# Soft-capped attention and a squared-ReLU MLP in one kernel: pads that set addresses, smaller weight loads, and decode work moved between engines and stages

## The chip, the cores and the metric

The kernel runs on one core of one Trainium2 chip. The metric is the device time of one execution in microseconds, less is better. TensorE does the matrix products, VectorE (DVE in the rows) and ScalarE (ACT) the elementwise work, GpSimd (POOL) and SyncE (SP) issue transfers. TensorE's granted clock is 1.00 (its 2.4 GHz level) over the whole span of the profiled execution.

## The reference, cut to what matters

Inputs are float32, except that the expert weights arrive as float64 words, which the kernel decodes itself.

```
q, k, v: (4, 12, 448, 64)                       # batch, heads, sequence, head size
scores = q @ k^T / 8;  scores = cap * tanh(scores / cap)
attn = exp(scores - max);  attn = attn / (sum(attn) + 1e-09)
x = (attn @ v), heads side by side              # (1792, 768)
h = relu(x @ w_in)                              # w_in  (768, 2048)
out = (h * h) @ w_out                           # w_out (2048, 768)
```

## The kernel before

The work has three stages, and inside a stage the order of the instructions on every engine is written out by hand.

**Attention.** 24 pairs of heads (a batch and two heads each), one iteration n of the loop in `tile_softcap_attention_mlp` for each, and a last one, n = 24, for what is left. In iteration n TensorE makes the scores of pair n (three products and, for every second pair, a fourth "half" one for two pairs), then, for pair n-1, the product with v (`pv_half`, `pv`, into the PSUM tile `pa`) and the sums of the row (`sums`, into `pb`). Both PSUM tiles exist once, so `pv_half` of a pair waits until `evac` of the pair before has copied `pa` away. ScalarE does tanh and exp. VectorE adds the exps (`add_p`, `add_p3`), transposes q and k (`turn_kq`), copies the sums out (`take_sums`), adds the guard 1e-9 to them and takes the reciprocal (`invert`), scales (`normalise`) and copies `pa` out (`evac`). The sums travel in a chain: `take_sums` copies them from PSUM, a transfer of SP gathers them into `cmp`, `invert` works on that small tile, SP stores it to DRAM, and `spread` on POOL loads it back over all partitions, three iterations later; `normalise` then multiplies. For the first two batches (pairs 0 to 11) `normalise` also splits its result into a rounded high part (a cast, line 503) and a low part (a subtraction, line 504).

**Weights inside the attention.** Column f of w_in (128 of its 2048 columns) is loaded by one transfer of 768 KB (`fetch_w`) and decoded in six steps: size and rest on ScalarE, clip, shift, sign and total on VectorE (lines 40 to 48); then its two halves are split into high and low operands (lines 557 and 558). `early_work` is a generator that yields after every step; the loop takes one step in an iteration from n = 4 and two from n = 10. Four columns are decoded there, three of them also split.

**First product.** Sixteen columns of w_in times x, as a Strassen scheme on blocks: for each pair of columns p seven products, each of 18 matmuls of 448 columns, all on line 345. Left operands are weights in the pool `w`. The moving operands x lie in five pools: B11 and B21 in `xab` (also products 1 and 2), B22 in `xg0` (product 3), T2 in `xg1` (product 6), B12 and later T1 in `xg2` (product 5), T3 and T4 in `xf` (products 7 and 4). A list scheduler (`Plan`) with written costs and due times puts the instructions of this stage in order; the rooms it gives out (raw tiles, decoded tiles, operands) are tokens. Columns 2 and 3 enter it as already decoded tiles.

**Second product.** Strassen again: 49 products of 24 matmuls of 384 columns on line 1124, with the squared h loaded back from DRAM (`load_a`), split into operands (lines 1113 and 1114) two products ahead, and fetched five products ahead (`LEAD`).

**Addresses.** Pools are laid out one behind the other. A pad (`shift`) is a tile that is never used and only moves what comes after it. `lctx` holds `xab`; `rctx` holds a pad, then `w`, a pad, `xf`, and further pools up to `xg0`; `xg1` and `xg2` are laid from the other end of the memory, behind `pad3`; the operand pool of the second product likewise, behind `pad4`. Tiles in these pools are whole multiples of 256 bytes in each partition, so that the distance between an x tile and a left operand, taken modulo 256 bytes, is the same for all tiles of a pool. In the layout before, x minus left operand is 192 for `xab`, 64 for `xf` and `xg0`, and 32 for `xg1` and `xg2`; in the second product it is 160 and 64.

## Time and profile before

| | |
|---|---|
| time, median of 3 runs | 597.59 us (596.75 to 599.28) |
| profiled execution: its time, its span | 595.01 us, 593.5 us |
| TensorE busy | 580.0 us (98%) |
| weight loads busy | 458.5 us (77%) |
| VectorE busy | 472.9 us (80%) |
| ScalarE busy | 375.5 us (63%) |
| GpSimd busy | 156.0 us (26%) |

The span runs from the first to the last instruction of the profiled execution; about 1.5 us of its own time lie outside. Attention ends at 172.6 us, where the first matmuls of the first product start; the second product runs from 384.2 to 588.4 us. Busy shares are averages over the three stages, which have different limits, so each stage has to be read alone. A busy TensorE isn't TensorE at its fastest: the distance from one matmul's start to the next one's is read from the timeline.

### The profile page before, as it was taken

The page shows a single profiled execution, that of the slowest core. Times are in us where ns is not written, and L with a number is a line of the kernel's source. Part 1 is how long each engine was busy: PE and PEld are TensorE (multiplying, and loading weights), DVE is VectorE, ACT ScalarE, POOL GpSimd, SP SyncE. Part 2 cuts the span into 40 slices and gives each one's busy share as a digit, 9 for nine tenths or more (in the row PEclk, how much of TensorE's full clock was granted, in tenths as well). Part 3 has the DMA queues.
Part 4 walks back from the last instruction along what each step waited for, and adds up shares of the span by engine and source line. Part 5 has one row for each costly group of instructions (what it writes and reads, how often), then busy time and mean ns, then how long its engine had stood idle before and what let it go on. Part 6 is the DMA issues. An engine that isn't in the chain of part 4 may idle for free.

```text
span 593.5 us, 9080 instructions
## 1 busy us (share of the span) xinstructions
PE 580.0 (98%) x3286; PEld 458.5 (77%) x3286; DVE 472.9 (80%) x646; ACT 375.5 (63%) x428; POOL 156.0 (26%) x245
## 2 busy tenths in 40 slices
PE   8998999999999999999999999999999999999996
PEld 5333333333348999999999999999999999999996
DVE  2878999999979898898787877734999998676661
ACT  5999788889976887686765757554833643323230
POOL 8687977777421000120211112100000000000000
PEclk9999999999999999999999999999999999999999
DMA  9999978979216233888878768979799618555611
GB/s 134 133 187 187 166 132 161 156 126 186 76 45 196 86 119 126 276 269 269 254 235 287 245 209 338 284 248 343 192 308 300 155 42 231 165 143 157 174 40 45
DMA packets 138678, 110.18 MB, mean 186 GB/s; under 512 B 53408, under 2 KB 127648, under 8 KB 138624
## 3 DMA queue, kind: packets, MB, share of 16 engines
q1 hardware_dynamic: 125088, 71.86, 48.0%
q0 software_dynamic: 12000, 37.39, 23.1%
q8 instruction: 27, 0.44, 0.4%
q10 hardware_dynamic: 1536, 0.27, 0.3%
q14 instruction: 27, 0.22, 0.2%
HBM read 82.84 MB, written 26.56 MB: 184 GB/s over the span
## 4 chain that ended last, share of the span: by engine, by line
PE 42%; issue 32%; DMA 8%; POOL 7%; DVE 6%; ACT 2%; SPq 2%; DVEq 0%; POOLq 0%
PE po L1124 30%; PE pa L455 4%; PE sc L397 4%; POOL g_dram L700 3%; DMA kqn<-in_k_dram 2%; POOL w_dram L1013 2%; PE pa L439 2%; POOL kqn L354 2%; DMA a<-g_dram 2%; ACT p L415 1%; DVE add L430 1%; DMA vn<-in_v_dram 1%; DMA kqn<-in_q_dram 1%; DVE kq L390 1%; PE pb L448 1%
## 5 line engine op out<-in xcount | busy, mean ns | idle before, releaser
L1124 PE MATMUL po<-th,gh 128*128 128x384 f32 x728 | 189.8, 336 | 0.0
L1124 PE MATMUL po<-th,gl 128*128 128x384 f32 x392 | 131.8, 336 | 0.2 <-DVE gl L1114 0.2
L1124 PEld LDWEIGHTS po<-th,gh 128*128 128x128 f32 x728 | 131.8, 188 | 0.0
L1113 ACT CAST gh<-a 128x1024 fp32r<-128x1024 f32 x47 | 49.4, 1051 | 96.7 <-PE po L1124 76.4
L345 PE MATMUL hps<-xt,op 128*128 128x448 f32 x450 | 93.9, 365 | 0.0
L345 PEld LDWEIGHTS hps<-xt,op 128*128 128x128 f32 x450 | 84.3, 187 | 7.0
L415 ACT ACTIVATE p<-sc 128x896 f32<-128x896 f32 x84 | 73.2, 909 | 19.6 <-PE sc L397 19.5
L1114 DVE TENSOR_TENSOR gl<-a,gh 128x1024 fp32r<-128x1024 f32 x47 | 57.5, 1222 | 23.2 <-ACT gh L1113 23.2
L1124 PEld LDWEIGHTS po<-th,gl 128*128 128x128 f32 x392 | 73.7, 188 | 0.5 <-DVE gl L1114 0.5
L423 ACT ACTIVATE p<-p 128x1792 f32<-128x1792 f32 (+1 forms) x48 | 72.5, 1510 | 1.4
L345 PE MATMUL hps<-xs,op 128*128 128x448 f32 x324 | 68.3, 365 | 0.0
L345 PEld LDWEIGHTS hps<-xs,op 128*128 128x128 f32 x324 | 60.6, 188 | 6.1 <-ACT p L415 0.7
L397 PE MATMUL sc<-kq 64*128 64x448 f32 x288 | 60.7, 554 | 0.5 <-DVE qks L530 0.5
L354 POOL DMA_DIRECT2D kqn<-in_k_dram x92 | 59.0, 647 | 7.4 <-DVE cmp L473 2.3
L455 PE MATMUL pa<-p,vn 128*64 128x448 f32 x288 | 59.4, 548 | 0.0
L397 PEld LDWEIGHTS sc<-kq 64*128 64x128 f32 x288 | 25.7, 186 | 34.6 <-issue 24.0
L345 PE MATMUL hps<-xh,op 128*128 128x448 f32 x168 | 49.6, 363 | 0.0
L379 POOL DMA_DIRECT2D vn<-in_v_dram x48 | 35.4, 741 | 31.9 <-PE pa L455 30.1
L455 PEld LDWEIGHTS pa<-p,vn 128*64 128x64 f32 x288 | 18.5, 136 | 30.9 <-issue 30.9
L48 DVE CUSTOM_DVE_ANT_0 wf<-wraw,wf 128x1536 uint16<-128x1536 uint16 x32 | 30.4, 951 | 5.6 <-ACT wraw L43 3.1
L1137 DVE TENSOR_TENSOR osb<-s,po 128x384 f32<-128x384 f32 x27 | 14.9, 552 | 25.0 <-PE po L1124 25.0
L40 ACT ACTIVATE wf<-wraw 128x768 f32<-128x768 f32 x32 | 29.0, 907 | 8.0 <-DMA w_dram<-wf 6.0
(95 smaller groups left out, 842.3 us busy)
## 6 DMA issues: line engine op xcount, KB each, us to landing
a<-g_dram SPq DMA_DIRECT2D x56, 512.0 KB
wraw<-in_moe_w_in_dram SPq DMA_DIRECT2D x16, 768.0 KB
wraw<-in_moe_w_out_dram SPq DMA_DIRECT2D x16, 768.0 KB
g_dram<-r POOLq DMA_DIRECT2D x18, 448.0 KB, 5.6
g_dram<-u POOLq DMA_DIRECT2D x14, 448.0 KB, 3.6
w_dram<-wf POOLq DMA_DIRECT2D x16, 384.0 KB, 6.4
vn<-in_v_dram POOLq DMA_DIRECT2D x48, 112.0 KB, 4.4
e<-rd POOLq DMA_DIRECT2D x48, 112.0 KB, 3.3
```

The costliest lines, as they stand in the source:

```text
L40: size=lambda: nc.scalar.activation(out=magf, in_=high.bitcast(F32), func=ACTF.Abs, scale=2.0 ** 16),
L48: total=lambda: V.tensor_tensor(out=mag, in0=mag, in1=low, op=ALU.add),
L345: nc.tensor.matmul(out=out, lhsT=w, rhs=x[:, j], start=start and c == 0 and s == 0, stop=stop and c == NHALF - 1 and s == 2, skip_group_ch ...
L354: queue.dma_start(out=kqn[n % NKQ][32 * a:32 * a + 32, i], in_=x)
L379: nc.gpsimd.dma_start(out=vn[n % NKV][r, at:at + NS], in_=x[i::2].rearrange("t r d -> r t d"))
L397: nc.tensor.matmul(out=sc[:, h, :S], lhsT=kt[r, keys(n, h, u)], rhs=qt[r], start=True, stop=True)
L415: nc.scalar.activation(out=p, in_=probs[n, u][:, :, :S], func=ACTF.Tanh, scale=by["qks"])
L423: nc.scalar.activation(out=p, in_=p, func=ACTF.Exp, scale=by["cap"])
L455: nc.tensor.matmul(out=pvs[n, 0][r], lhsT=vn[n % NKV][:, v_slot(n, h, u)], rhs=p[:, h], start=False, stop=(u == NU - 1))
L1113: last["act"] = nc.scalar.copy(out=hi, in_=x)
L1114: last["dve"] = nc.vector.tensor_sub(out=lo, in0=x, in1=f32(hi))
L1124: last["mm"] = nc.tensor.matmul(out=po, lhsT=w[:, c], rhs=m[:, cols], start=(c == 0 and i == 0), stop=(c == HF - 1 and i == 2))
```

## The change

- Two pads grow or are added: `pad0` of 32 words (128 bytes) ahead of `xab`, and `pad1` from 16 to 112 words ahead of `w`. `pad3` shrinks by 8 words (32 bytes), `pad4` grows by 32 words (128 bytes). x minus left operand becomes 64 modulo 256 for all five pools of the first product; in the second product it stays at 160 and 64, with the operands themselves at other places.
- w_in's first four columns are loaded in six transfers of 128 KB each, two in an iteration, from the iterations in `FETCH` (6, 9, 14, 18), in place of one of 768 KB.
- Three columns are decoded in the attention, not four, from n = 9 on, with the number of steps for each iteration in the list `DECODE`. Column 3 is only loaded there; its decode becomes part of the first product's plan.
- The guard is added in `take_sums`, by the instruction that copies the sums out of PSUM; the addition of line 472 goes.
- The cast of line 503 becomes a ScalarE copy one iteration later (`split_high`), and the subtraction follows it (`split_low`).
- B22's split is done for both batches at once in place of one by one.
- Six in place of five tiles of h are loaded ahead of the second product, and those of its first 14 products are fetched two products earlier. The pools of that stage wait for single tiles instead of whole pools when they reuse memory (`by_tile`).

```diff
+    shift(lctx, "pad0", 32)
     xab = lctx.enter_context(tc.tile_pool(name="xab", bufs=NQ))
-    shift(rctx, "pad1", 16)
+    shift(rctx, "pad1", 112)
...
     def take_sums(n):
         e = ep.tile([P, S], F32, tag="es", name="es", bufs=1)
-        nc.vector.tensor_copy(out=e, in_=pvs.pop((n, 1)))
+        nc.vector.tensor_scalar(out=e, in0=pvs.pop((n, 1)), scalar1=guard, scalar2=None, op0=ALU.add)
...
     def invert(n):
         cmp = rds[n]
-        nc.vector.tensor_scalar(out=cmp, in0=cmp, scalar1=guard[:NC], scalar2=None, op0=ALU.add)
         nc.vector.reciprocal(out=cmp, in_=cmp)
...
         nc.vector.tensor_mul(out=x, in0=e[:, 0], in1=e[:, 1])
-        if half:
-            return
-        if b == 0:
-            t = xab.tile([P, 2, 2, S], F32R, tag="x", name="xs")
-            xs.setdefault(("B11", "B21")[i], {})[c] = t[:, 0], t[:, 1]
-        hi, lo = (t[:, b] for t in xs[("B11", "B21")[i]][c])
-        nc.vector.tensor_copy(out=hi, in_=x)
-        nc.vector.tensor_sub(out=lo, in0=x, in1=hi.bitcast(F32))
+        if not half:
+            whole[n] = x, ("B11", "B21")[i], c, b
+
+    def split_high(n):
+        if n in whole:
+            x, name, c, b = whole[n]
+            if b == 0:
+                t = xab.tile([P, 2, 2, S], F32R, tag="x", name="xs")
+                xs.setdefault(name, {})[c] = t[:, 0], t[:, 1]
+            nc.scalar.copy(out=xs[name][c][0][:, b], in_=x)
+
+    def split_low(n):
+        if n in whole:
+            x, name, c, b = whole.pop(n)
+            hi, lo = (t[:, b] for t in xs[name][c])
+            nc.vector.tensor_sub(out=lo, in0=x, in1=hi.bitcast(F32))
...
+    def fetch_early(n):
+
+        for f, at in enumerate(FETCH):
+            if at <= n < at + NHALF:
+                if n == at:
+                    raws[f] = new_raw(scr, 2)
+                for c in (2 * (n - at), 2 * (n - at) + 1):
+                    nc.sync.dma_start(out=raws[f][:, c * P:(c + 1) * P], in_=w_in[c * P:(c + 1) * P, f * P:(f + 1) * P])
...
-    START, DEEP = 4, 3
+    START, DEEP = 9, 3
+    FETCH = 6, 9, 14, 18
+    DECODE = 1, 2, 2, 1, 2, 3, 2, 2, 1, 2, 3, 2, 2, 3, 2, 0
...
         if n >= START:
-            decode_on(1 + (n >= 10))
+            decode_on(DECODE[n - START])
+        split_high(n - 5)
...
             take_sums(n - 1)
-            fetch_wanted()
+            fetch_early(n)
             pv(n - 1)
...
             normalise(n - 4)
+        split_low(n - 5)
         if old:
             evac(n - 1)
...
-    shift(tctx, "pad3", 24, side="right", **by_tile)
+    shift(tctx, "pad3", 16, side="right", **by_tile)
...
-        raw=[(0.0, i, p) for i, p in enumerate((left, left, right))],
-        f=[(0.0, i, right) for i in range(2)],
+        raw=[(0.0, i, p) for i, p in ((1, left), (2, right))],
+        f=[(0.0, 0, left), (0.0, 1, right), (0.0, 3, right)],
...
+    columns[1, 1] = round_column(True, 3, due[6, 1] - 5.0, 40.0, raw3)
...
-    d22 = [split_x("B22", c, [one(x22[c], j) for j in range(2)], due["u", 0, 1], [(), (normal[c],)], xg[0])
-           for c in range(NHALF)]
+    d22 = [split_x("B22", c, [wide(x22[c])], due["u", 0, 1], [(normal[c],)], xg[0]) for c in range(NHALF)]
...
-        shift(lctx, "pad4", 24, side="right", **by_tile)
+        shift(lctx, "pad4", 56, side="right", **by_tile)
...
-    for i in range(LEAD):
+    for i in range(NRAW):
         first_a(i)
...
+        coming = [x for x in PRODUCTS if x[0] != 1 or x[1] >= NRAW]
...
-            for lead, step in ((LEAD, fetch), (3, blend)):
-                if z + lead < N:
-                    step(*PRODUCTS[z + lead])
+            while coming and PRODUCTS.index(coming[0]) <= z + (LEAD + 2 if coming[0][0] < 3 else LEAD):
+                fetch(*coming.pop(0))
+            if z + 3 < N:
+                blend(*PRODUCTS[z + 3])
```

## Rows read from the trace of the kernel before

**Rows 1.** Busy time by stretch: stretch, length, then each engine's busy us (instructions), clock, DMA share, GB/s.

```profile
46.50:126.30 79.80, 74.47 (x490) 26.27 (x488) 76.19 (x126) 69.36 (x65) 61.09 (x93) 1.00 0.90 157
126.30:172.60 46.30, 46.30 (x306) 16.41 (x304) 41.26 (x69) 42.60 (x41) 26.19 (x40) 1.00 0.58 113
180.30:222.00 41.70, 41.70 (x207) 38.54 (x206) 39.96 (x54) 33.07 (x46) 4.02 (x7) 1.00 0.41 137
384.20:588.40 204.20, 204.01 (x1177) 203.66 (x1176) 148.03 (x150) 81.65 (x80) 0.54 (x1) 1.00 0.65 185
```

**Rows 2.** Timeline (start, length, instruction), TensorE: scores of n = 6, 17, 20, 21; sums.

```profile
46.55 2.53 PE L397 MATMUL sc<-kq 64*128 64x448 f32 x12
...
126.32 2.53 PE L397 MATMUL sc<-kq 64*128 64x448 f32 x12
...
145.95 2.53 PE L397 MATMUL sc<-kq 64*128 64x448 f32 x12
...
152.99 2.53 PE L397 MATMUL sc<-kq 64*128 64x448 f32 x12
...
156.36 0.59 PE L448 MATMUL pb<-add,ones 128*32 128x224 f32 x8
```

**Rows 3.** Timeline, VectorE in attention; brackets: idle time before and what ended it.

```profile
55.41 0.63 DVE L496 TENSOR_TENSOR xf<-e 128x448 f32<-128x448 f32 x1 [1.73 <-DMA e<-rd]
...
92.67 1.08 DVE L430 TENSOR_TENSOR add<-add,p 128x896 f32<-128x896 f32 x1
...
95.26 0.48 DVE L558 TENSOR_TENSOR op<-wf,op 128x384 fp32r<-128x384 f32 x1
...
99.35 1.08 DVE L430 TENSOR_TENSOR add<-add,p 128x896 f32<-128x896 f32 x1
```

**Rows 4.** Groups by line and shape: count, then busy us, mean ns, idle before.

```profile
L472 DVE TENSOR_SCALAR cmp<-cmp,guard 32x28 f32<-32x28 f32 x24 | 5.5, 231 | 1.6 <-DMA cmp<-es 1.6
L503 DVE CAST xs<-xf 128x448 fp32r<-128x448 f32 x12 | 5.2, 436 | 0.4
L749 ACT CAST xt<-xf 128x448 fp32r<-128x448 f32 x6 | 3.1, 563 | 2.9 <-DVE xf L496 2.9
L43 ACT ACTIVATE wraw<-wraw 128x768 uint32<-128x768 uint32 x32 | 29.2, 912 | 0.0
L44 DVE TENSOR_SCALAR wf<-wf 128x768 uint32<-128x768 uint32 x32 | 17.6, 551 | 0.8
L46 DVE SCALAR_TENSOR_TENSOR wf<-wraw,wf 128x768 uint32<-128x768 uint32 x32 | 30.6, 956 | 0.9
```

**Rows 5.** Timeline, ScalarE: the last exp of pair 20.

```profile
152.12 1.70 ACT L423 ACTIVATE p<-p 128x1792 f32<-128x1792 f32 x1
```

**Rows 6.** Timeline, TensorE in the first product, by runs of equal operands.

```profile
202.34 3.80 PE L345 MATMUL hps<-xs,op 128*128 128x448 f32 x18
...
256.90 3.76 PE L345 MATMUL hps<-xt,op 128*128 128x448 f32 x18
...
260.50 3.81 PE L345 MATMUL hps<-xs,op 128*128 128x448 f32 x18
264.15 7.52 PE L345 MATMUL hps<-xt,op 128*128 128x448 f32 x36
271.51 0.37 PE L345 MATMUL hps<-xh,op 128*128 128x448 f32 x1
271.72 0.36 PE L345 MATMUL hps<-xl,op 128*128 128x448 f32 x1
```

**Rows 7.** Timeline, VectorE after the attention: last `normalise`, last half of B22's split.

```profile
194.57 0.63 DVE L496 TENSOR_TENSOR xf<-e 128x448 f32<-128x448 f32 x1 [1.43 <-DMA e<-rd]
...
197.12 0.62 DVE L755 TENSOR_TENSOR xt<-xf,xt 128x448 fp32r<-128x448 f32 x1
```

**Rows 8.** Timeline, TensorE in the second product, its one wait.

```profile
409.37 0.34 PE L1124 MATMUL po<-tl,gh 128*128 128x384 f32 x1
409.90 0.44 PE L1124 MATMUL po<-th,gl 128*128 128x384 f32 x1 [0.19 <-DVE gl L1114]
```

More of the change, by code (lines that the diff above doesn't have):

```diff
@@ L318, in tile_softcap_attention_mlp, with new_raw @@
     xs, xt = {}, {}
+    def new_raw(pool, bufs):
+        return pool.tile([P, DM], U64, tag="wraw", name="wraw", bufs=bufs)
     def fetch_w(pool, f, first, bufs):
[L321 removed]
+        raw = new_raw(pool, bufs)
         if first:
@@ L545, in early_work @@
     def early_work():
-        raw = fetch_w(scr, 0, True, 2)
-        yield
-        for f in range(4):
-            coming = []
-            if f < 3:
-                wanted.append((coming, f + 1))
+        for f in range(3):
             mag = held[f] = new_f(scr, 2)
-            yield from decode(nc, raw, mag)
-            for o in range(2 * (f < 3)):
+            yield from decode(nc, raws[f], mag)
+            for o in range(2):
                 ops[f, o] = new_op()
@@ L558, in early_work @@
                 yield nc.vector.tensor_sub(out=ops[f, o][:, 1], in0=side(mag, o), in1=ops[f, o][:, 0].bitcast(F32))
-            raw = coming and coming[0]
-    def fetch_wanted():
-        while wanted:
-            into, f = wanted.pop()
-            into.append(fetch_w(scr, f, True, 2))
-    wanted = []
+    def fetch_early(n):
[5 more added lines that the diff above has]
+                    nc.sync.dma_start(out=raws[f][:, c * P:(c + 1) * P], in_=w_in[c * P:(c + 1) * P, f * P:(f + 1) * P])
+    raws = {}
     decoding = early_work()
@@ L768, in wide @@
         return lambda: [(x()[:], slice(0, 2))]
-    def one(x, j):
-        return lambda: [(x()[:, j], j)]
     def minus(at, out, a, b, *after):
@@ L783, in pe, with round_column @@
         return in_turn("pe", lambda prev: do("PE", cost, emit, prev, *after, lag=0.15, due=due[key], **kw))
-    def round_column(first, f, at, early):
-        h = SimpleNamespace()
+    def round_column(first, f, at, early, raw=None):
+        h = SimpleNamespace(raw=raw)
         def fetch():
@@ L796, in size @@
             h.steps.size()
-        h.fetch, here = transfer("SP", fetch, 768, due=at - 16.0, ready=at - early, take="raw")
+        if raw:
+            h.fetch, here = taken("raw", 0, left), None
+        else:
+            h.fetch, here = transfer("SP", fetch, 768, due=at - 16.0, ready=at - early, take="raw")
         add_size = lambda prev: do("ACT", 0.86, size, here, prev, due=at - 6.0, take="f")
@@ L826, in tile_softcap_attention_mlp @@
     left_ops = {(1, "A11"): ready_op(2, 0), (1, "A12"): ready_op(2, 1)}
-    columns = {(1, e): SimpleNamespace(f=held[2 + e], size=taken("f", 2 + e, left), done=None) for e in range(2)}
+    columns = {(1, 0): SimpleNamespace(f=held[2], size=taken("f", 2, left), done=None)}
+    raw3 = raws[3]
     def round_pair(p, e):
@@ L1019, in tile_softcap_attention_mlp @@
         part(f, WSTART + (END - WEND - WSTART) * (f + 1) / NF)
-    raws, later = {}, {}
+    raws.clear()
+    later = {}
     n_raw, n_op, n_bank = [0], [0], [0]
@@ L1094, in tile_softcap_attention_mlp @@
         mctx.enter_context(tc.manual_schedule(engines={E.PE, E.Activation, E.DVE, E.SP}))
-        ps_o = mctx.enter_context(tc.tile_pool(name="ps_o", bufs=2, space=PSUM, side="right"))
-        ps_o2 = mctx.enter_context(tc.tile_pool(name="ps_o2", bufs=6, space=PSUM))
-        tw2 = mctx.enter_context(tc.tile_pool(name="tw2", bufs=14))
+        ps_o = mctx.enter_context(tc.tile_pool(name="ps_o", bufs=2, space=PSUM, side="right", **by_tile))
+        ps_o2 = mctx.enter_context(tc.tile_pool(name="ps_o2", bufs=6, space=PSUM, **by_tile))
+        tw2 = mctx.enter_context(tc.tile_pool(name="tw2", bufs=14, **by_tile))
         mctx.enter_context(tc.tile_pool(name="opad", bufs=1)).tile([P, 48], F32, name="opad")
-        opp2 = mctx.enter_context(tc.tile_pool(name="opp2", bufs=1))
-        ob = mctx.enter_context(tc.tile_pool(name="ob", bufs=3))
-        later["raw2"] = mctx.enter_context(tc.tile_pool(name="raw2", bufs=2))
-        sv = mctx.enter_context(tc.tile_pool(name="sv", bufs=2 * HT))
+        opp2 = mctx.enter_context(tc.tile_pool(name="opp2", bufs=1, **by_tile))
+        ob = mctx.enter_context(tc.tile_pool(name="ob", bufs=3, **by_tile))
+        later["raw2"] = mctx.enter_context(tc.tile_pool(name="raw2", bufs=2, **by_tile))
+        sv = mctx.enter_context(tc.tile_pool(name="sv", bufs=2 * HT, **by_tile))
         opp = later["opp"]
```

4 lines of the change are left out of this document (2 added, 2 removed).

## The prediction

> **What bounds the kernel now.** I read first the busy time by stretch, then the timeline of TensorE for the starts of its matmuls, then the timelines of the engines that it waits for. TensorE is busy for 98% of the span, so little can be won: the time it idles, and the time by which its matmuls stand further apart than they need.
>
> In the attention it idles in one part only. From n = 6 to n = 16 (46.5 to 126.3 us) it is busy 74.5 of 79.8 us; from n = 17 on it is busy throughout [rows 1]. The starts of the scores give the price: the even iteration 20 takes 152.99 - 145.95 = 7.04 us; 17 to 19, two odd ones and an even one, take 126.32 to 145.95, 19.63, so an odd one 6.29 [rows 2]. Six even and five odd ones are 73.7 us; n = 6 to 16 took 126.32 - 46.55 = 79.8. So 6.0 us are lost there. The engine that is late is VectorE, busy 76.2 us of that stretch, more than TensorE's 73.7, while it has 41.3 of 46.3 us afterwards [rows 1]: up to n = 15 `normalise` also casts and subtracts. One such cycle, from one `add_p3` to the next, is 99.35 - 92.67 = 6.68 us with one decode step of 0.48 in it [rows 3]; without decode about 6.25 of the 6.67 that an average iteration allows, and decode adds up to 1.5 in an iteration. Its lateness reaches TensorE through `evac`, which `pv_half` waits for. One part of it is a transfer: at 55.41 `normalise` had waited 1.73 us for the sums to be spread [rows 3], just after two transfers of 768 KB of weights.
>
> In the first product TensorE never idles, but its matmuls of one size have two paces: 18 with x in `xg0` take 260.50 - 256.90 = 3.60 us (200 ns each), 18 in `xab` 3.65, and 36 in `xg1` and `xg2` 7.36 (204 ns) [rows 6]. In the second product 1176 matmuls take 204.2 us, 173.6 ns each, with one wait [rows 1, 8].
>
> **Guard in the sums' copy.** The addition of 231 ns goes from VectorE [rows 4]; the copy out of PSUM becomes an addition over the same 128x448 elements. No row shows that form from PSUM; between nothing (a copy and an addition pass the same elements) and the guard's whole 231 ns given back, I take nothing, since the scalar addition on line 44 takes no longer per element than a copy does. 11 iterations win 2.5 us of VectorE.
>
> **Cast to ScalarE.** VectorE loses 436 ns in each of 10 iterations of the stretch, 4.4 us; one subtraction more falls into it (n = 16), 0.6 us back. ScalarE pays 563 ns [rows 4], some 0.46 of it alone, as successive instructions overlap by about 0.1 (two tanh of 0.91 take 1.71). The copy stands ahead of the last tanh and exp of its iteration in ScalarE's queue; behind these wait `add_p3` and `pv_half` of the next one. Its input is ready since the iteration before.
>
> **Decode later and for three columns.** In n = 6 to 16 VectorE had 15 decode steps by the order of the loop, now 11; the four fewer are a total (as long as a sign, 0.96 [rows 4]), a subtraction of 0.48 [rows 3] and two casts of some 0.35 (448 columns take 0.44 [rows 4]), 2.1 us. ScalarE gets one step more there, 0.9.
>
> So VectorE's sum falls from 76.2 to 76.2 - 2.5 - 4.4 + 0.6 - 2.1 = 67.8 us, below TensorE's 73.7. **ScalarE is next**: 69.4 [rows 1] + 11 x 0.46 + 0.8 = 75.3, a little above TensorE. It may end late by some margin: the last exp of pair 20 ends at 153.82, 0.83 after the scores of n = 21 start [rows 2, 5]; `add_p3` (1.08 [rows 3]) must follow before the sums are taken, 156.36 - 152.99 = 3.4 us after an odd iteration's start [rows 2], so up to about 2.1 us nothing waits. Walked by iteration with 0.46 for a cast and 0.8 for a decode step, its end lies at 1.3 after n = 8, at 2.1 to 2.2 after n = 10, 14, 15 and 16, and below elsewhere. That is the margin itself, so some stall stays; where the exp is so late VectorE starts late too, and n = 12 pays for n = 11's 1.4 us of decode with about 0.45. I keep 0.8 us of stall in all: the attention wins 6.0 - 0.8 = 5.2 us. The ends are 0 (ScalarE takes the whole place of VectorE) and 6.0.
>
> **Smaller transfers.** The same bytes, in 128 KB pieces; SP issues two more in each of twelve iterations, behind the gather of the sums; queued behind them are the next q loads, which are wanted four iterations on. The wait of 1.73 [rows 3] should go; it is inside the 6.0 us. The first column's last pieces are issued at the end of n = 8 and read in n = 9 about 5 us later; were they late, ScalarE would hold up tanh and exp by as much, once.
>
> **x and left operands at other distances.** `pad1` puts 384 bytes more between `xab` and `w`: 192 becomes 64 modulo 256. `pad3` moves `xg1` and `xg2` by 32 bytes: 32 becomes 64. `xf` and `xg0` stay at 64, the distance of the quick pace. 324 matmuls read `xab` (18 groups): 18 x 0.05 = 0.9 us at most. Products 6 and 5 of seven pairs: 7 x (7.36 - 7.20) = 1.1 us. 36 more read B12 in `xg2`: 0.2. Sum 2.2; the rows round, I take 2.1, from 0 (the pace follows something else) to 2.2. The second product keeps its distances: nothing. The rows show two paces for one size of matmul at a full clock [rows 1, 6].
>
> The Trainium skill, "TensorE: Matmul & The Clock Gate", section "Back-to-back issue gap", gives the spacing by columns alone (columns over the clock, plus 2.5 ns) and names no address. By it this part would be worth nothing, and the sum would be 2.1 us smaller. The rows disagree with it, since equal matmuls differ by 4 ns in them.
>
> **Column 3 in the first product.** VectorE gets 0.55 + 0.55 + 0.96 + 0.96 = 3.0 us (clip, shift, sign, total), of which the total was there already, ScalarE two steps, 1.8 [rows 4]. Until 222 us VectorE is busy 40.0 of 41.7 us [rows 1]. The last half of B22's split ended at 197.74; its readers are the last matmuls ahead of 202.34, so about 4 us were left [rows 6, 7]. Split as a whole it is wanted 1.8 us sooner and takes 0.5 longer: some 1.7 us are left, less 0.5 for TensorE's quicker pace, plus what the wait of 1.43 for the spread sums gives back, since one weight load fewer is queued beside it. The 2 us more of VectorE's work are due later than this, but an instruction that is running isn't stopped, so up to 1 us of it can get ahead. I take no stall; the bounds are 0 and 1.5 us.
>
> **Start of the second product.** The h tiles come earlier, and the wait at 409 us (0.53 in place of 0.17 between two matmuls [rows 8]) goes: 0.4 us. It can cost something only where SP's queue stands longer on a full buffer; the output stores behind it aren't waited for.
>
> **Sum.** 5.2 + 2.1 + 0.4 = 7.7 us. On the profiled execution 595.0 becomes 587.3, its span 593.5 becomes 585.8. The median of the runs is 2.6 us above the profiled one: 597.6 - 7.7 = **589.9 us**.
>
> **Rivals.** (a) ScalarE takes VectorE's place and can't be kept busier than VectorE was, 76.2 of 79.8 us: 75.3 / 0.955 = 78.8, a gain of 1.0 in the attention: 594.1. For it: its sum is above TensorE's. Against it: it has 42.6 of 46.3 us after n = 17 with no stall at all [rows 1], and a wait for a transfer was part of VectorE's idle time. (b) The pace doesn't follow the distance modulo 256: 592.0. Against it: `xg0` and `xf`, which alone have 64, are the quick ones. (c) Column 3 makes VectorE late for B22 or for the first operands of the pairs: 1.5 us, 591.4. (d) On the other side: in the second product left operands and x move together (128 bytes each). If what counts is where each lies, not the distance, its 1176 matmuls can slow down. From 7.7 / 1176 = 6.5 ns each the kernel is slower than before; the first product's widest single distance in the rows is 271.72 - 271.51 = 210 ns, 10 above its quick pace [rows 6], so 11.8 us at most: 601.7. Against it: the second product reads x at two distances (160 and 64) and its 173.6 ns are a mean over both, only 14 above the 160 that 384 columns take at 2.4 GHz, as 200 is 13 above the 187 of 448 columns. (e) The small transfers and the guard do nothing for TensorE because both were off its path: part of (a)'s time.
>
> **How the numbers follow.** My forecast 0.52, (a) with (e) 0.24, (b) 0.08, (c) 0.12, (d) 0.04. The range goes from the full gain with no stall left (8.7 us, 588.9), less a microsecond for the scatter of the runs, to (a) with the same: 587.8 to 595.3. A measurement can tell about 0.5%, 3.0 us: faster than 594.6 is the forecast, (b), (c) and most of (a), 0.80; within it the rest of (a) and cases that add up, 0.16; slower (d), 0.04.
>
> **What would show it.** The scores of n = 6 and of n = 17 would lie about 74.5 us apart, with ScalarE busy near its whole and VectorE's idle time ended by exp. Runs of 18 matmuls of all pools would take 3.60 us. No TensorE idle time around 200 and 409 us. The prediction is wrong if that stretch stays over 77 us, if the runs of `xab` stay at 3.65, or if the second product's 1176 matmuls no longer take 204 us.

## The result and the profile after

| | before | after |
|---|---|---|
| time, median | 597.17 us (595.23 to 599.28) | 586.83 us (586.40 to 587.41) |
| profiled execution: its time, its span | 595.01, 593.5 us | 587.03, 585.4 us |
| TensorE / VectorE / ScalarE busy | 580.0 / 472.9 / 375.5 us | 576.9 / 463.8 / 380.2 us |

The ratio is 0.9828, 95% interval 0.9806 to 0.9851: faster by 10.3 us. The forecast was 589.9 us with a range from 587.8, so the time lies 1.0 us below the range. The span of the profiled execution came out as forecast (585.8, measured 585.4); the median did not: it fell by 10.3 us where 7.7 were forecast. Where the other 2.6 us come from is the main question below.

First the busy time by stretch of the kernel after (columns as in [rows 1]): n = 6 to 16, n = 17 to 23, the first product's start, the second product.

```profile
46.70:120.90 74.20, 73.82 (x492) 26.18 (x490) 65.86 (x98) 71.57 (x76) 58.75 (x89) 1.00 1.01 170
120.90:167.20 46.30, 46.30 (x307) 16.42 (x305) 43.15 (x66) 44.35 (x42) 26.88 (x42) 1.00 0.64 125
174.80:216.50 41.70, 41.70 (x210) 39.10 (x209) 40.17 (x51) 34.34 (x44) 4.04 (x7) 1.00 0.40 137
376.50:580.20 203.70, 203.70 (x1177) 203.68 (x1176) 150.35 (x152) 81.96 (x80) 0.54 (x1) 1.00 0.60 184
```

Against [rows 1], n = 6 to 16 went from 79.8 to 74.2 us; VectorE, the fullest engine there, has 65.9 of them in place of 76.2. TensorE is busy throughout the other three.

The timeline of TensorE shows what is left: scores of n = 6, 12, 13 and 17.

```profile
46.68 2.53 PE L401 MATMUL sc<-kq 64*128 64x448 f32 x12
...
86.70 2.53 PE L401 MATMUL sc<-kq 64*128 64x448 f32 x12
94.19 2.53 PE L401 MATMUL sc<-kq 64*128 64x448 f32 x12
...
120.88 2.53 PE L401 MATMUL sc<-kq 64*128 64x448 f32 x12
```

From 46.68 to 120.88 are 74.20 us, 0.5 above the floor of 73.7. Of this 94.19 - 86.70 - 7.04 = 0.45 lie in n = 12.

In the first product all pools have the quick pace now (same timeline; xt of `xg0`, xs of `xab`, then 36 of `xg1` and `xg2`):

```profile
200.12 3.76 PE L349 MATMUL hps<-xt,op 128*128 128x448 f32 x18
203.72 3.76 PE L349 MATMUL hps<-xs,op 128*128 128x448 f32 x18
207.32 7.36 PE L349 MATMUL hps<-xt,op 128*128 128x448 f32 x36
```

Start to start 3.60 us each for 18, where `xab` had 3.65 and the 36 are recorded as 7.36 in place of 7.52 [rows 6]. From its second unit to the start of the second product the first product took 376.52 - 174.80 = 201.7 us, 2.2 less than before; the second product 203.7 in place of 204.2.

Groups by line and shape of the kernel after give the new costs (columns as in [rows 4]):

```profile
L469 DVE TENSOR_SCALAR es<-pb,guard 128x448 f32<-128x448 f32 x24 | 16.2, 676 | 11.3 <-PE pb L452 11.1
L515 DVE TENSOR_TENSOR xs<-xf,xs 128x448 fp32r<-128x448 f32 x12 | 7.4, 617 | 0.9 <-ACT xs L509 0.9
L509 ACT CAST xs<-xf 128x448 fp32r<-128x448 f32 x12 | 6.7, 556 | 0.0
L443 PE MATMUL pa<-p,vn 64*64 64x448 f32 x96 | 23.3, 562 | 1.1 <-ACT p L427 0.7 <-DVE e L464 0.4
```

The copy alone, in the kernel before:

```profile
L465 DVE COPY es<-pb 128x448 f32<-128x448 f32 x24 | 14.5, 604 | 4.8 <-PE pb L448 4.8
```

The copy with the guard takes 676 ns, some 70 more than the copy alone; the cast on ScalarE 556; `pv_half` waits 1.1 us in the whole kernel, 0.7 for exp and 0.4 for `evac`.

### The profile page after: what moved, and what is told of

The parts are those of the page before. It is cut to its first block, busy times and chain, and to the rows that moved or that the text cites. A ratio compares the mean times of both kernels' runs of the same rounds, so it can differ in the third digit from the quotient of the medians.

```text
span 585.4 us, 9055 instructions
## 1 busy us (share of the span) xinstructions
PE 576.9 (99%) x3286; PEld 458.2 (78%) x3286; DVE 463.8 (79%) x607; ACT 380.2 (65%) x437; POOL 156.1 (27%) x245
## 4 chain that ended last, share of the span: by engine, by line
PE 93%; DMA 2%; DVE 2%; ACT 1%; issue 0%; SPq 0%; POOL 0%; ACTq 0%; DVEq 0%; POOLq 0%
PE hps L349 35%; PE po L1141 35%; PE pa L459 9%; PE sc L401 8%; PE pa L443 3%; PE pb L452 2%; PE sc L409 1%; DMA cap_sb<-in_cap_dram 1%; DMA cmp<-es 1%; ACT p L427 1%; ACT p L419 1%; DMA wraw<-in_moe_w_in_dram 1%; DVE es L469 0%; SPq L472 0%; POOL kqn L358 0%
## 5 line engine op out<-in xcount | busy, mean ns | idle before, releaser
L349 PE MATMUL hps<-xt,op 128*128 128x448 f32 x450 | 92.4, 362 | 0.0
L1141 PEld LDWEIGHTS po<-th,gl 128*128 128x128 f32 x392 | 73.7, 188 | 0.0
```

The source lines that it names most:

```text
L349: nc.tensor.matmul(out=out, lhsT=w, rhs=x[:, j], start=start and c == 0 and s == 0, stop=stop and c == NHALF - 1 and s == 2, skip_group_ch ...
L1141: last["mm"] = nc.tensor.matmul(out=po, lhsT=w[:, c], rhs=m[:, cols], start=(c == 0 and i == 0), stop=(c == HF - 1 and i == 2))
```

## The experiments

All times stand beside the kernel before, which over all comparisons had a median of 596.6 us, its executions lying between 593.9 and 601.2 (85 of them; before_again adds one of 603.5). "n = 6 to 16" is the distance from the scores of n = 6 to those of n = 17; a "loss" is what an iteration takes beyond 7.04 us (even) or 6.29 us (odd). A "landing" is the end of a transfer, for which an engine can wait. shift_all, three_back_again and the two kernels with other distances ran once, so they have no interval.

### What makes the kernel before slow and uneven

**The kernel before, unchanged (before_again).**

> The kernel before, unchanged, to see what differs between its executions. The first profiled one took 595.0 us while six executions lay between 595.2 and 599.3; the changed kernel's six lie within 1.0 us. Theory 1 (the scatter is attention's): its executions differ in the stretch from the scores of n = 6 to those of n = 17, 79.8 us in the first trace, by as much as they differ in time, and the other stretches (start to n = 6: 46.6; n = 17 to the first product: 46.3; first product from its second unit 203.9; second product 204.2) agree within 0.3 us. Rival: that stretch stays at 79.8 and the rest of the time moves elsewhere (start, end, or a lower granted clock).

595.5 us (594.9 to 603.5); the profiled execution 595.5, its n = 6 to 16 80.4 us. From n = 9 to 16 it loses what the first trace lost (3.7 and 3.5 us), and the stages outside n = 6 to 16 agree within 0.3 us; n = 6 to 8 lose 3.0 us in place of 2.6, n = 7 alone 2.7 in place of 1.4. VectorE's timeline there:

```profile
56.19 0.62 DVE L496 TENSOR_TENSOR xf<-e 128x448 f32<-128x448 f32 x1 [2.57 <-DMA e<-rd]
```

The same wait for the spread sums as in [rows 3], 2.57 in place of 1.73 us. So a landing is a term that varies. The two profiled executions lie only 0.4 us apart, and none of the long ones of this kernel was profiled.

**Weight loads from another queue (w_on_act).** SP's queue in the trace of before suggested a cause. Starts and durations of issues, the weight load ahead, the q loads, the store of the reciprocals:

```profile
47.25 0.41 SPq L323 DMA_DIRECT2D wraw<-in_moe_w_in_dram  x1
47.70 4.82 SPq L354 DMA_DIRECT2D kqn<-in_q_dram  x5
52.65 1.19 SPq L475 DMA_DIRECT2D rd<-cmp  x1
```

Five q loads take 4.82 us to issue behind a weight load, and the store, from which the spread starts, stands behind them. The edit moves the weight loads to ScalarE's queue.

```diff
-            nc.sync.dma_start(
+            (nc.scalar if f < 4 else nc.sync).dma_start(
```

> The kernel before, with the 768 KB loads of w_in's first four columns issued by ScalarE's queue in place of SyncE's. In the traces of before and of the pads alone, the five q loads that follow such a load in SP's queue take 4.1 to 5.3 us to issue (2.5 in the changed kernel), the store of the reciprocals stands behind them, the spread of the sums goes out late, and VectorE waits 1.7 to 2.6 us for it at n = 7. Theory P (the order of SP's queue): the q loads behind no weight load issue in about 2.5 us, the wait for the spread sums is below 0.4 us, n = 6 to 16 take 78.0 to 78.7 us and the median is 593.5 to 594.5. Theory T (the transfers share the same engines, whoever issues them): the q loads still take over 4 us, the wait stays above 1.5 us and the median is 595.5 to 596.5.

597.5 us (594.9 to 598.4), ratio 1.0005 [0.9983, 1.0026], a microsecond above what theory T expected and three above theory P. In its trace SP's five q loads took longer still, with no weight load in their queue:

```profile
48.41 7.04 SPq L354 DMA_DIRECT2D kqn<-in_q_dram  x5
```

VectorE waited for the gathered sums:

```profile
54.92 0.23 DVE L472 TENSOR_SCALAR cmp<-cmp,guard 32x28 f32<-32x28 f32 x1 [2.48 <-DMA cmp<-es]
```

That the weight load stands ahead in SP's queue is not the cause. The theory of shared transfer engines is left standing; this run doesn't show it.

**Guard, cast and decode's pace all back in the changed kernel (three_back), and the same once more (three_back_again).**

```diff
-        nc.vector.tensor_scalar(out=e, in0=pvs.pop((n, 1)), scalar1=guard, scalar2=None, op0=ALU.add)
+        nc.vector.tensor_copy(out=e, in_=pvs.pop((n, 1)))
...
-            nc.scalar.copy(out=xs[name][c][0][:, b], in_=x)
...
+            nc.vector.tensor_copy(out=hi, in_=x)
...
-    START, DEEP = 9, 3
-    FETCH = 6, 9, 14, 18
-    DECODE = 1, 2, 2, 1, 2, 3, 2, 2, 1, 2, 3, 2, 2, 3, 2, 0
+    START, DEEP = 5, 3
+    FETCH = 2, 6, 12, 18
+    DECODE = 1, 1, 1, 1, 1, 2, 2, 2, 2, 2, 2, 2, 2, 2, 2, 2, 2, 1, 0, 0
```

(The addition in `invert` comes back too.)

> The changed kernel with guard, cast and the pace of the decode all as before, but its small transfers, its pads, its third stage and column 3 in the first product kept. Theory 2 (any one relief can be missed, not all): VectorE is late again, 3 to 5 us of stall in n = 6 to 17, scatter of 2 to 4 us, 590 to 592 us. Rival (the small transfers are what counts): 587 to 588 us.

590.2 us (589.5 to 595.2), 0.9901 [0.9866, 0.9935]: 3.4 us of the gain gone, and the executions spread over 5.7 us. The profiled one was the longest, 595.2.

> The kernel three_back once more, unchanged: its executions lay between 589.5 and 595.2 us, and the one with a profile was the longest. In that one VectorE waited 5.4 us in n = 6 to 12 for the gathered sums and was busy 77.4 of 82.6 us. If late landings, paid in full by an engine without slack, make the scatter of before as well, an execution of 589.5 to 591 us shows VectorE busy the same 77.4 us in n = 6 to 16, a stretch of 77.0 to 78.5 us, and waits for the gathered sums of under 1.5 us in all. If the waits stay near 5 us and the time is short, the scatter is somewhere else.

589.6 us. The busy time of n = 6 to 16, of the long execution and then of the short one:

```profile
46.70:129.30 82.60, 74.37 (x490) 26.26 (x488) 77.39 (x129) 70.12 (x66) 62.90 (x94) 1.00 1.02 155
```

```profile
46.30:123.70 77.40, 74.37 (x492) 26.31 (x490) 74.78 (x127) 69.98 (x66) 60.74 (x92) 1.00 1.01 161
```

TensorE's work is the same to the last digit; the stretch is 5.2 us longer. VectorE's timeline of the long one, its waits for landings in this stretch until 70 us:

```profile
46.90 0.23 DVE L476 TENSOR_SCALAR cmp<-cmp,guard 32x28 f32<-32x28 f32 x1 [1.30 <-DMA cmp<-es]
...
54.67 0.40 DVE L476 TENSOR_SCALAR cmp<-cmp,guard 32x28 f32<-32x28 f32 x1 [1.68 <-DMA cmp<-es]
...
68.84 0.35 DVE L476 TENSOR_SCALAR cmp<-cmp,guard 32x28 f32<-32x28 f32 x1 [1.12 <-DMA cmp<-es]
```

With those not shown they add up to 5.4 us, against 1.8 in the short execution (a little over the 1.5 expected), so they make 3.6 of the 5.2 us. VectorE's busy time, expected equal, is 2.6 us less in the short one. Executions of one kernel differ, for the most part, by how late the sums land.

**The kernel before with all tiles moved by 32 bytes (before_moved).** The moved kernels further down (shift_all) showed the same transfers at less cost, which led to this one: distances between operands as before, only the places differ.

```diff
+    shift(lctx, "pad0", 8)
     xab = lctx.enter_context(tc.tile_pool(name="xab", bufs=NQ))
...
-    shift(tctx, "pad3", 24, side="right", **by_tile)
+    shift(tctx, "pad3", 16, side="right", **by_tile)
...
-        shift(lctx, "pad4", 24, side="right", **by_tile)
+        shift(lctx, "pad4", 16, side="right", **by_tile)
```

> The kernel before with all its tiles moved by 32 bytes (a pad of 8 words ahead of xab, pad3 and pad4 8 words smaller); every distance between operands stays as it was. In the two traces of the changed kernel moved so, the same transfers took the DMA engines less time (up to 60 us into the span 31.6 and 35.7% of their time on the two largest queues against 45.8 and 51.0, and from 10 to 26 us a busy share of 0.64 to 0.67 against 1.27): tiles that transfers write began 32 bytes behind a multiple of 64, and there at a multiple of 64. Theory T (late landings from busy transfer engines, paid by VectorE without slack, make the scatter of before): the waits of VectorE for landings in n = 6 to 8 fall below 0.5 us, n = 6 to 16 take 77.5 to 78.8 us, the median is 592.0 to 594.0 and the executions lie within 2 us. Rival (the scatter has another cause, and only the start gains): n = 6 to 16 stay at 79.5 to 81, the first scores start 0.7 to 1.0 us earlier, the median is 595.3 to 596.0 and the executions scatter by 4 us as before.

590.8 us (590.1 to 591.9), 0.9912 [0.9890, 0.9933]: 4.9 us from 32 bytes, even more than expected, and executions within 1.7 us. Busy time by stretch, early attention (the last two columns are DMA share and GB/s) and n = 6 to 16; first of before, then of before moved:

```profile
10.00:26.00 16.00, 14.59 (x94) 4.85 (x94) 11.12 (x18) 15.77 (x17) 12.15 (x19) 1.00 1.30 151
```

```profile
10.00:26.00 16.00, 14.33 (x94) 4.81 (x92) 10.59 (x15) 15.80 (x16) 11.96 (x19) 1.00 0.65 139
45.40:122.00 76.60, 74.15 (x490) 26.25 (x488) 75.08 (x125) 69.35 (x65) 59.05 (x91) 1.00 0.72 160
```

The DMA share halves, at 139 GB/s in place of 151. By queue, from the start to 60 us, before and then before moved:

```profile
q1 hardware_dynamic: 23365, 4.25, 56.6%
q0 software_dynamic: 2509, 5.13, 52.2%
```

```profile
q1 hardware_dynamic: 23917, 4.32, 40.4%
q0 software_dynamic: 2776, 5.71, 38.4%
```

More packets and bytes, in three quarters of the time. VectorE's longest wait for a landing in n = 6 to 16 is 0.28 us, n = 7 loses nothing, and n = 6 to 16 take 76.65 us: 2.95 above the floor, all of it from n = 10 on, with no late landing, so VectorE's own overload. The first scores start at 6.59 us in place of 7.56. So the 79.8 us of before were the floor, some 3 us of VectorE's own work and some 3 us of late landings, and the last vary from one execution to the next. Of the 5.0 us between the two spans 1.2 lie ahead of n = 6, 3.1 in n = 6 to 16 and 0.5 in the second product, whose one wait [rows 8] is gone. The rival (another cause) falls.

### The parts of the change

**The pads alone, in the kernel before (pads_alone).**

```diff
+    shift(lctx, "pad0", 32)
     xab = lctx.enter_context(tc.tile_pool(name="xab", bufs=NQ))
-    shift(rctx, "pad1", 16)
+    shift(rctx, "pad1", 112)
...
-    shift(tctx, "pad3", 24, side="right", **by_tile)
+    shift(tctx, "pad3", 16, side="right", **by_tile)
...
-        shift(lctx, "pad4", 24, side="right", **by_tile)
+        shift(lctx, "pad4", 56, side="right", **by_tile)
```

> The kernel before with the four pads of the change and nothing else. Distance theory: the first product shrinks by 2.1 to 2.2 us (203.9 to 201.7), 18 matmuls of every pool take 3.60 us; attention loses its 6 us or more as before, so about 595 us median with the same scatter of 3 to 4 us. Rival (the pace follows something else of the change): first product 203.9, 597 us.

595.4 us (592.7 to 597.2), 1.0001 [0.9984, 1.0018]. The first product took 202.2 us in place of 203.9; 201.7 was expected, and a wait of 0.22 us at 370 us lies in it. The profiled execution lost the gain in n = 7. VectorE's wait for the spread sums, then TensorE's timeline and granted clock (last column but two) there:

```profile
57.12 0.63 DVE L497 TENSOR_TENSOR xf<-e 128x448 f32<-128x448 f32 x1 [2.51 <-DMA e<-rd]
```

```profile
59.49 0.59 PE L440 MATMUL pa<-p,vn 64*64 64x448 f32 x2 [2.96 <-ACT p L416]
...
59.89 0.81 PE L440 MATMUL pa<-p,vn 64*64 64x448 f32 x2
```

```profile
59.40:62.00 2.60, 2.50 (x18) 0.73 (x20) 2.57 (x5) 1.59 (x2) 2.33 (x4) 0.63 0.98 174
62.00:66.00 4.00, 4.00 (x18) 1.45 (x16) 3.46 (x7) 0.02 (x1) 3.70 (x6) 0.81 0.74 154
```

After VectorE's 2.51 us TensorE idled for 2.96 us, its granted clock fell to 0.63 and 0.81 (part of the time at 1.2 GHz), and matmuls of 0.54 us took 0.81. n = 7 lost 4.6 us. Alone, the pads gave nothing in the median, and scatter doesn't explain that: 2 us less would be a ratio of 0.9966, outside the interval. Attention paid them back in the profiled execution (81.8 us for n = 6 to 16 in place of 79.8), and it seems in others: the mean granted clock of the execution was 0.996 or less in 6 of the 10 executions, against 5 of 25 of the kernel before beside them. Why such waits came more often with the pads isn't shown.

**The changed kernel without its pads (pads_back).** The same diff the other way round.

> The changed kernel with its four pads as before, all else changed. Distance theory: only the first product moves, 201.7 us becomes 203.9, runs of 18 matmuls in xab take 3.65 us and 36 in xg1 and xg2 7.36; 589.0 us with a scatter of 1 us. Rival (the pads had no part; pads_alone showed no gain in time): 586.8 us.

589.2 us (588.8 to 590.2): 2.3 us more than after. The first product takes 203.94 us again. The pads are worth 2.2, as forecast.

**Guard and cast alone, in the kernel before (relief_alone).** The hunks of `take_sums`, `invert`, `split_high` and `split_low`.

> The kernel before with only the guard in the sums' copy and the cast on ScalarE; large transfers, early decode, four columns and all pads as before. Theory 3 (the scatter is VectorE's lack of room, which hands every late landing to TensorE): with a cycle of 5.4 us in place of 6.2 most late landings are absorbed; stalls after n = 9 fall from about 4 us to under 1, n = 7 keeps at most 1.5; 591 to 592 us, scatter at most 2 us. Rival (the scatter comes with the two large loads between 45 and 48 us, whoever has room): n = 7 keeps its 1.5 to 4.6 us, runs scatter by 3 us or more, 592 to 594 us.

592.0 us (591.5 to 596.7), 0.9937 [0.9909, 0.9965]. n = 9 to 16 lose 0.3 us in all in place of 3.5; n = 6 to 8 still lose 2.5, with waits for landings of 1.82, 1.10 and 0.51 us, and the executions spread over 5.2 us where theory 3 expected 2 at most. So half of that theory fails: VectorE has room here (69.9 us busy of 76.6), and the late landings are handed on all the same. For n = 6 to 8 the rival fits (SP issues the two large loads at 36.4 and 47.9 us).

**Small transfers alone, in the kernel before (small_alone).** The loads of the four columns as in `fetch_early`, from n = 2, 6, 12 and 17.

> The kernel before with its first four columns loaded in 128 KB transfers, two in an iteration, from n = 2, 6, 12 and 17, decoded when the kernel before does it; all else as before. Theory 1a (the large transfers cause the scatter and the wait of 1.73 us at 55 us): the stretch n = 6 to 17 takes about 78 us, runs lie within 1.5 us of one another, about 594.5 us. Theory 1b (VectorE, with no time to spare, turns any late landing into lost time, whatever its size): the stretch stays near 79.5 to 82 us and runs still scatter by 3 to 4 us, 596 to 597 us.

594.1 us (593.0 to 596.8), 0.9971 [0.9950, 0.9993]. The loss in n = 7 is gone, but waits for the gathered sums appear (0.91, 0.69, 0.56 us), and n = 10 and 11 lose 1.4 and 1.1. The scatter stays near 4 us. Neither theory has this: a part of the loss and of the time goes, the scatter doesn't.

**Four steps back, one at a time, in the changed kernel.** The loads in one transfer each (one_transfer):

```diff
-                for c in (2 * (n - at), 2 * (n - at) + 1):
-                    nc.sync.dma_start(out=raws[f][:, c * P:(c + 1) * P], in_=w_in[c * P:(c + 1) * P, f * P:(f + 1) * P])
+            if n == at:
+                raws[f] = fetch_w(scr, f, True, 2)
```

> The changed kernel with each early column again in one 768 KB transfer, issued at the first of its three iterations. Theory 1b: VectorE now has room, so late landings are absorbed: n = 6 to 17 within 0.5 us of the changed kernel's 74.2, scatter about 1 us, 587 us. Theory 1a: waits for the spread sums come back, 1.5 to 2 us, and with them a scatter of 2 us or more: 588.5 to 590 us.

586.9 us (586.8 to 587.4); n = 12 loses 1.2 us in the profiled execution. The cast on VectorE again (cast_back):

> The changed kernel with the high part cast on VectorE again, ahead of the subtraction; guard, loads and decode as changed. Theory 2 (several small reliefs, of which VectorE needs only some): VectorE's cycle is 6.05 us without decode, below TensorE's 6.67, so at most 0.5 us more stall in n = 6 to 17 than the changed kernel's 0.5; 587 us, scatter about 1 us. Rival (the cast's move is what freed VectorE): stalls of 2 to 4 us come back, 589 to 591 us, with scatter.

586.7 us (586.4 to 587.9). The guard in `invert` again (guard_back):

> The changed kernel with the guard added again on the small tile ahead of the reciprocal, and a plain copy of the sums. Theory 2: 0.2 us more of VectorE in an iteration, some 0.2 to 0.4 us of stall in all, around n = 12: 587.1 us. Rival (the chain of the sums is what was late): 588.5 us or more.

587.7 us (587.2 to 589.0). The earlier pace of decode, the diff of START, FETCH and DECODE above (decode_early):

> The changed kernel with its three columns decoded at the pace of the kernel before (one step from n = 5, two from n = 10), loads of 128 KB from n = 2, 6 and 12. Theory 2: the later start isn't needed, since VectorE's cycle is 5.4 us without decode and at most 6.8 with it; the stall at n = 12 (0.45 us in the changed kernel) goes, and others stay under 0.4: 586.5 us. Rival (the quiet iterations up to n = 8 are needed): 1 to 2 us of stall come back, 588 us.

587.6 us (586.6 to 588.2). Each costs 0 to 0.9 us by itself; guard, cast and pace together cost 3.4 (three_back). These three give VectorE room, and any one of them can be missing: the spread stays at 1.4 to 1.8 us (four executions each), where guard and cast alone (relief_alone) and the small transfers alone left 5.2 and 3.8.

### What sets the pace of the matmuls

**Other distances (distance_map, distance_two).** The first has pads of 16, 64, 32, 56 and 24 words (pad0 to pad4) and 64 in the second product's `opad`, the second 0, 40, 56, 40 and 56.

> The changed kernel with other pads: x minus left operand is 0 for xab, 128 for xf and xg0, 160 for xg1 and xg2, and in the second product 224 and 0 in place of 160 and 64. Distance theory: the pace differs by pool as the distance does; 64 took 200 ns a matmul, 192 took 202 to 203, 32 took 204 to 205; 0 and 160 are expected slower than 200, 128 between 200 and 203. The second product should stay at 203.7 us if it doesn't feel distances, and grow by up to 6 us if it does.

> The changed kernel with its pads set for other distances (x minus left operand modulo 256): 96 for xab, 224 for xf and xg0, 128 for xg1 and xg2; 32 and 64 in the second product in place of 160 and 64. So far 448-column matmuls took 200.0 ns each at 64, 202.0 at 160, 202.9 at 192, 204.0 at 128, 204.9 at 0 and 204.9 at 32. If the distance alone sets the pace, xg1 and xg2 take 204 ns as xf and xg0 did at 128; 96 lies between 32 and 128 and should take 200 to 204.5; 224 lies between 192 and 0 and should take 203 to 205. The first product then takes 1.5 to 3.5 us longer, the second up to 1 us longer, as 32 was the slowest distance of the first. If a pool's place counts and not its distance, xg1 and xg2 at 128 differ from 204 by over 1 ns.

590.8 and 593.6 us; the first products took 205.2 and 206.0 us, 3.5 and 4.3 longer than after (1.5 to 3.5 were expected of the second kernel). Spacing of the 448-column matmuls at a granted clock of 1.00, by x minus left operand modulo 256 bytes, from these two kernels, after and pads_back; mean, least and greatest over groups of 18 without a wait (the expectations' figures are means over all, so they differ by up to 0.7):

| distance | 0 | 32 | 64 | 96 | 128 | 160 | 192 | 224 |
|---|---|---|---|---|---|---|---|---|
| mean, ns | 204.4 | 204.9 | 200.1 | 205.2 | 203.9 | 202.0 | 202.3 | 203.8 |
| least | 202.6 | 204.4 | 200.0 | 205.1 | 203.3 | 200.0 | 201.9 | 203.3 |
| greatest | 206.1 | 206.7 | 200.7 | 205.6 | 204.5 | 206.8 | 202.7 | 204.4 |

TensorE's timeline of distance_map (xs at 0, xt at 160) and of distance_two (xt at 128):

```profile
230.32 3.81 PE L349 MATMUL hps<-xs,op 128*128 128x448 f32 x18
233.97 7.38 PE L349 MATMUL hps<-xt,op 128*128 128x448 f32 x36
...
244.86 3.87 PE L349 MATMUL hps<-xs,op 128*128 128x448 f32 x18
```

```profile
233.93 7.50 PE L349 MATMUL hps<-xt,op 128*128 128x448 f32 x36
```

64 is the quickest, and with all pools at 64 (after) every group takes 200.0; in pads_back, where other pools lie at other distances, groups of `xf` at 64 took up to 200.7. At 128 `xf` and `xg0` in the one kernel and `xg1` and `xg2` in the other take the same 203.3 to 204.5, which speaks for the distance and against the pool's place. But the distance alone doesn't set the pace elsewhere: at 0 the products of one pool differ (3.81 and 3.87 above, and so by turns from 219 to 347 us), and at 160 groups took 206.4 to 206.8 before 216 us and 200.0 to 200.9 later. 96 is the slowest, not between its neighbours as expected. In the second product 384 columns take 173.3 ns at 64 and 160, 173.4 at 224, 174.2 at 0 and 176.5 at 32, where this product lasted 206.2 us in place of 203.7 (up to 1 us more was expected): it feels the distance too.

**All operands moved by 32 bytes, distances kept (shift_all, shift_again).**

```diff
-    shift(lctx, "pad0", 32)
+    shift(lctx, "pad0", 40)
...
-    shift(tctx, "pad3", 16, side="right", **by_tile)
+    shift(tctx, "pad3", 8, side="right", **by_tile)
...
-        shift(lctx, "pad4", 56, side="right", **by_tile)
+        shift(lctx, "pad4", 48, side="right", **by_tile)
```

> The changed kernel with everything that TensorE reads in the first and the second product moved by 32 bytes, so that all distances stay (64 in the first product, 160 and 64 in the second). Distance theory: 201.7 us for the first product and 203.7 for the second, as in the changed kernel. Rival (it counts where an operand lies): the first product takes 204 us or more.

585.4 us, one execution. The pace of every pool is that of after (200.0 and 173.3 ns).

> The kernel shift_all once more, timed: the changed kernel with all operands of both products moved by 32 bytes and every distance kept. Its one execution took 585.4 us, 1.0 below the shortest of the changed kernel (586.4 to 587.4), but its stages last as long as there (n = 6 to 16 74.2 us, first product 201.7, second 203.7); only its first scores start earlier, at 6.6 us in place of 7.5. If the place of the operands does nothing and the start scatters, the median is 586.5 to 587.2 and the first scores start at 7.4 to 7.7. If the place gives something, the median stays at 585.2 to 585.9.

585.7 us (585.4 to 586.2), 0.9810 [0.9791, 0.9829]. It stays below every execution of the kernel after, so the place gives something, but not to the matmuls: the first scores start at 6.90 us, where all unmoved kernels had 7.4 to 7.9, since the first q tile lands earlier (VectorE starts on it at 6.20 in place of 6.97 us). The whole gain lies ahead of n = 6, which starts 1.0 us earlier. Early attention of after, then of this kernel:

```profile
10.00:26.00 16.00, 14.83 (x94) 4.80 (x94) 11.50 (x17) 15.80 (x16) 12.05 (x19) 1.00 1.27 151
```

```profile
10.00:26.00 16.00, 14.24 (x94) 4.56 (x88) 10.45 (x13) 15.80 (x16) 11.96 (x19) 1.00 0.64 138
```

As in before_moved the DMA share halves. This is the shortest of all kernels here, 1.1 us below after and 11 us below before.

### The rest in n = 12

**One decode step moved from n = 11 (smooth).** (The list puts it into n = 12; the expectation's words name n = 13.)

```diff
-    DECODE = 1, 2, 2, 1, 2, 3, 2, 2, 1, 2, 3, 2, 2, 3, 2, 0
+    DECODE = 1, 2, 1, 2, 2, 3, 2, 2, 1, 2, 3, 2, 2, 3, 2, 0
```

> The changed kernel, with one decode step moved from n = 11 to n = 13 (DECODE 1, 2, 1, 2, 2, 3 in place of 1, 2, 2, 1, 2, 3), so that no odd iteration of 6.29 us carries 1.4 us of VectorE's decode. Theory (the 0.45 us at n = 12 is paid for n = 11's steps): the start of n = 13's scores comes 7.04 us after n = 12's in place of 7.49, the attention is 0.4 us shorter and the time about 586.4. Rival (the step costs the same where it lands): n = 14 is late by 0.3 to 0.5 us in its place and the time doesn't change.

587.9 us (586.6 to 589.9), no better. TensorE's timeline, scores of n = 11 to 13, and VectorE's in n = 12:

```profile
80.01 2.53 PE L401 MATMUL sc<-kq 64*128 64x448 f32 x12
...
86.73 2.53 PE L401 MATMUL sc<-kq 64*128 64x448 f32 x12
...
93.77 2.53 PE L401 MATMUL sc<-kq 64*128 64x448 f32 x12
```

```profile
91.56 0.32 DVE L476 RECIPROCAL cmp<-cmp 32x28 f32<-32x28 f32 x1 [0.83 <-DMA cmp<-es]
91.80 0.88 DVE L46 SCALAR_TENSOR_TENSOR wf<-wraw,wf 128x768 uint32<-128x768 uint32 x1
92.72 0.96 DVE L48 CUSTOM_DVE_ANT_0 wf<-wraw,wf 128x1536 uint16<-128x1536 uint16 x1
```

n = 12 takes 7.04 us, its 0.45 is gone; but sign and total now follow one another behind a wait of 0.83, and n = 13 loses 0.79 and n = 11, after a wait of 1.22, 0.43. The rival comes nearer: the step costs where it lands, though more than it said, and late landings have a part in it. The executions spread over 3.3 us, so the small spread of the kernel after isn't safe against a change of one step.

## Why the prediction was right and wrong

**The step that failed is the last of the sum**, "The median of the runs is 2.6 us above the profiled one", carried over to the changed kernel. It took the 2.6 us as a constant of the kernel. They come from the scatter of the kernel before, whose profiled execution was one of its short ones, and the change removes the scatter: its profiled execution lies 0.2 us above its median. So an offset of 2.6 measured -0.2, while the sum on the profiled execution (587.3) measured 587.03. Part of the 2.6 was chance as well: 597.6 was the median of three executions, and over 85 it is 596.6, an offset of 1.5.

What stood behind this was mis-sized as well: of the 6.0 us lost in n = 6 to 16, the working gave one wait of 1.73 [rows 3] to a transfer. before_moved shows half of the loss, 79.77 - 76.65 = 3.1 us, to be late landings; three_back and its repetition show that the waits for them differ by 3.6 us between executions, and the stretch by 5.2, and pads_alone that a long one costs the granted clock as well. An engine at 76 of 80 us hands late landings on in full: before waited 2.4 us for them in n = 6 to 8 and lost 2.6. One at 66 of 75 hands on a part: smooth waited 4.0 us and lost 1.2. Room alone isn't enough (relief_alone); which parts together take the spread away wasn't tried one by one. The low end of the range allowed one microsecond for scatter, where the removed landings were worth more.

**Attention.** 5.2 forecast, 5.6 measured; "about 74.5 us apart" became 74.2. n = 12 paid 0.45, the size that was walked, though VectorE's wait of 0.56 us for the gathered sums at 77.5, which the walk didn't have, may be a part of it; of the other 0.35 of stall 0.05 came. VectorE's 67.8 were 65.9: the stretch is no longer late and holds one `normalise` and one subtraction fewer (10 each, 11 before), where the sum had one subtraction more, 1.9 us in all. ScalarE's 75.3 were 71.6: one exp fewer falls into the stretch (1.7 us), and the rest (2 us) is overlap: the durations of its instructions there add up to 77.1 us against 72.6 before, its busy time to 71.6 against 69.4, as instructions without a gap between them overlap in the record. Rival (a), 594.1, needed ScalarE at 95% with stalls; it is at 96% with 0.5 us of stall. "In the attention it idles in one part only" missed the start: TensorE is busy 14.6 of 16 us from 10 to 26 us, and shift_again won 1.0 us ahead of n = 6. Of the sums two are slightly off: 6.0 + 2.2 + 0.4 is 8.6, not 8.7, and 6.68 - 0.48 is 6.20, not 6.25.

**Guard.** "I take nothing" was slightly wrong: 0.07 us for each copy against 0.23 given back. **Cast:** 0.46 of 0.56 alone, as taken (the next tanh starts 0.45 after it); undone by itself it costs nothing, since VectorE has room. **Small transfers:** inside the 6.0, right: alone they gave 1.9 us (small_alone); in the changed kernel one large transfer is no worse. With guard_back's 0.9 us, rival (e) falls. **Distances:** 2.1 forecast, 2.2 measured, also by pads_back. Rival (b) falls. The Trainium skill, "TensorE: Matmul & The Clock Gate", section "Back-to-back issue gap", gives the spacing by columns alone; the runs disagree, with group means of 200.0 to 206.8 ns for the same 448 columns. **Column 3:** no stall, as taken: the wait of 1.43 for the spread sums [rows 7] is gone in VectorE's timeline after,

```profile
186.71 0.61 DVE L499 TENSOR_TENSOR xf<-e 128x448 f32<-128x448 f32 x1
```

and TensorE is busy throughout that stretch; rival (c) falls. **Second product:** 0.4 forecast, 0.5 measured. That the earlier loads of h did it isn't shown: pads_back has the 0.5 without the pads, but before_moved and pads_alone have it without the earlier loads. Rival (d) (its operands' places) falls, since moved places with equal distances keep 173.3 ns; had the distances not been kept, 32 would have cost 2.5 us (distance_two).

## What to carry to other kernels

Before adding an offset between profiled time and median to a forecast, ask what makes executions differ: where an engine without slack waits for landings, a change that ends most of those waits takes the spread away (here 3 to 7 us became 1.0) and lowers the median by more than the span of a short execution shows. Relief of that engine alone needn't do it (relief_alone kept 5.2 us). Several reliefs of one engine can be worth little each when undone and much together, so undo them together as well. Where a pad moves tiles, look at the DMA share as well as at the matmuls.

## What the runs showed of the hardware

By the layout of the pools, tiles that transfers write (q, k, v and weights) begin 32 bytes behind a multiple of 64 in each partition in all kernels but the moved ones, where they begin at a multiple of 64. There the DMA share from 10 to 26 us is 0.64 to 0.67 in place of 1.27 to 1.31, at 138 to 144 GB/s in place of some 151, and the kernel before gains 4.9 us. That the multiple of 64 decides, and not another property of the place, wasn't tried at other offsets; which of the tiles matter is open too.

The spacing of equal matmuls at full clock depends on the distance of their two operands modulo 256 bytes, by up to 3% in the means of the table above, without a plain order, and on something more, which differs between products and stretches (200.0 to 206.8 ns at 160, 200.0 to 200.7 at 64). What that is and why 64 is the quickest is open.
